# Sliding-window attention with adapters on one core: q and k laid out in 16-row runs, and PSUM handed out by the bank

## The chip, the cores and the metric

The kernel runs on one core of one Trainium2 chip. The metric is the device time of one execution in microseconds. Each execution has a state: "slow" when it lies over 1.5% above the fastest of the same kernel. The engines are called PE (matmuls; PEld is its weight load), ACT, DVE, POOL and SP, as the profile calls them. PE's results land in PSUM; the operands kT and qT of its matmuls lie in SBUF. "Granted clock" is the share of PE's full clock that the profile shows as granted.

## The reference, cut to what matters

```python
# q, k, v: (8 batches, 8 heads, 576 rows, 64)
scores = (q @ k.T) / 8                       # only |row - column| <= 32 survives the mask
attn   = softmax(where(mask, scores, -1e9))
x      = (attn @ v)                          # -> (8*576, 512), heads side by side
# then, per row of x: gate to the best 2 of 8 adapters of rank 16,
out    = x + sum over the 2 of  w * (x @ A[e]) @ B[e]
```

## The kernel before: the parts that matter here

The kernel keeps q and k transposed (64 head columns on partitions, two heads stacked on 128). It loads rows with a DMA that casts to f16, transposes on PE into PSUM, and copies PSUM to SBUF, q on DVE and k on ACT. Rows are loaded in runs of 18 (`NJ`), so a transpose of column block `j` gives every 18th row. The copies put the rows in order. For the score matmul, even and odd keys are kept apart (`v`), and the two stacked heads are interleaved key by key (`t`), with zeros in the other head's places.

```python
NJ, JC = 18, 6
S_t = [psum.tile([128, 2, 512], F32) for i in range(3)]   # 3 buffers of two banks
M_t = [psum.tile([128, 512], F32) for i in range(2)]      # 2 buffers of one bank: all transposes
qT = [const.tile([128, 64 + 4 * S], F16) for i in range(2)]
kT = [const.tile([128, 2, 2 * S, 2], F16) for i in range(2)]     # (v, key pair, t)

def f_q(b, c):      # PSUM -> SBUF on DVE, a third of a batch
    tp  = m16(...)[:, 0:128 * JC].rearrange("p (j r) -> p r j", j=JC)
    dst = qT[b % NQT][:, 32:32 + 4 * S].rearrange("p (r j) -> p r j", j=NJ)
    nc.vector.tensor_copy(out=dst[:, :, JC * c:JC * c + JC], in_=tp)

def f_k(b, c, t, eng):   # PSUM -> SBUF on ACT: 256 groups of 3 elements
    p0  = 64 * t
    tp  = m16(...)[p0:p0 + 64, 0:128 * JC].rearrange("p (h v r) -> p v r h", h=3, v=2)
    dst = kT[b % NKT][p0:p0 + 64, :, :, t].rearrange("p v (r h) -> p v r h", h=9)
    dst = dst[:, :, :, 3 * c:3 * c + 3]
    nc.scalar.copy(out=dst, in_=tp)
...
# A list scheduler in Python fixes the order of all instructions beforehand.
# Each task has an engine, an assumed duration (us), a due time and PSUM buffers:
T["ek", b, c, t] = plan.add("ACT", 0.85, f_k(b, c, t, "ACT"), base + 1 + 0.1 * c, ...)
```

After the scores, ACT takes the exp (`PT`), PE multiplies by v, DVE normalises, and the adapter part follows (transposes of x, gate, two matmuls, copy out).

The softmax here doesn't subtract the row's maximum and nothing guards it: scores larger than these inputs give would overflow.

## Time and profile before

| | before |
|---|---|
| time | 274.05 us (2 runs, 273.84 to 274.26) |
| PE / ACT / DVE busy | 63% / 55% / 42% of 272.8 us |
| kT copies on ACT | 48, 87.7 us in all |
| mean granted PE clock | 0.83 |

The first part of the page gives busy times, and the second one the busy tenths in 40 slices. From the page of the kernel before:

```profile
PE 170.6 (63%) x2312; PEld 120.9 (44%) x2312; DVE 115.2 (42%) x324; ACT 150.8 (55%) x125; POOL 64.4 (24%) x112
...
PE   0203196399529947399539947499439943798642
...
ACT  0007955972497419942696319943696349732413
...
PEclk9999999569956986569956986569959987599987
```

PE and ACT take turns: in seven of the ten slices where ACT shows 9, PE shows 2 to 4 and its clock 5 to 7. Next, groups of instructions (line, engine, operation, output<-input, shapes, count | busy us, mean ns of one | idle time before and what ended it), also from the page before:

```profile
L292 ACT COPY kT<-M 64x768 f16<-64x768 f16 x48 | 87.7, 1826 | 16.0 <-PE M L272 15.3
L322 ACT ACTIVATE PT<-S 128x1024 f16<-128x1024 f32 x36 | 36.8, 1023 | 46.7 <-PE S L312 42.5
...
L281 DVE COPY qT<-M 128x768 f16<-128x768 f16 x24 | 22.4, 951 | 0.1
...
L457 ACT COPY zT<-M 128x640 f16<-128x640 f16 x8 | 5.8, 724 | 22.8 <-PE M L450 22.8
```

A contiguous ACT copy of 640 elements (zT) takes 0.72 us, but the kT copy of 768 takes 1.83 us. The view of waits (who waited for whom: us in total, times, longest) says what PE stood still for:

```profile
PE M L272 <- DVE qT L281: 19.7, 10, 13.0
PE M L379 <- ACT kT L292: 17.0, 4, 5.0
...
PE M L272 <- ACT kT L292: 10.8, 5, 3.1
...
PE S L312 <- ACT kT L292: 8.2, 5, 6.1
```

### The profile page before, as it was taken

The page shows a single profiled execution, that of the slowest core. Times are in us where ns is not written, and L with a number is a line of the kernel's source. Part 1 is how long each engine was busy: PE and PEld are TensorE (multiplying, and loading weights), DVE is VectorE, ACT ScalarE, POOL GpSimd, SP SyncE. Part 2 cuts the span into 40 slices and gives each one's busy share as a digit, 9 for nine tenths or more (in the row PEclk, how much of TensorE's full clock was granted, in tenths as well). Part 3 has the DMA queues.
Part 4 walks back from the last instruction along what each step waited for, and adds up shares of the span by engine and source line. Part 5 has one row for each costly group of instructions (what it writes and reads, how often), then busy time and mean ns, then how long its engine had stood idle before and what let it go on. Part 6 is the DMA issues. An engine that isn't in the chain of part 4 may idle for free. (4 is left out here: it accounts for less than half of the span.)

```text
span 272.8 us, 5487 instructions
## 1 busy us (share of the span) xinstructions
PE 170.6 (63%) x2312; PEld 120.9 (44%) x2312; DVE 115.2 (42%) x324; ACT 150.8 (55%) x125; POOL 64.4 (24%) x112
## 2 busy tenths in 40 slices
PE   0203196399529947399539947499439943798642
PEld 0103074268414833288415833278316721487410
DVE  4883017018811680119801680128803750167430
ACT  0007955972497419942696319943696349732413
POOL 3898643009230041015410031015300000000000
PEclk9999999569956986569956986569959987599987
DMA  6839999009998182908695092909405004000135
GB/s 106 111 34 169 83 140 139 0 2 110 167 118 208 55 106 66 201 20 82 95 130 173 4 118 79 194 2 88 44 2 173 2 2 170 3 4 2 45 129 173
DMA packets 33960, 24.22 MB, mean 89 GB/s; under 512 B 25104, under 2 KB 25232, under 8 KB 33936
## 3 DMA queue, kind: packets, MB, share of 16 engines
q0 software_dynamic: 28688, 14.43, 49.8%
q1 hardware_dynamic: 5248, 9.44, 10.1%
q8 instruction: 18, 0.29, 0.5%
q14 instruction: 6, 0.05, 0.1%
HBM read 28.85 MB, written 9.44 MB: 140 GB/s over the span
## 5 line engine op out<-in xcount | busy, mean ns | idle before, releaser
L292 ACT COPY kT<-M 64x768 f16<-64x768 f16 x48 | 87.7, 1826 | 16.0 <-PE M L272 15.3
L212 POOL DMA_DIRECT2D vbd<-in_v_dram x64 | 38.8, 626 | 101.5 <-PE S L348 94.5
L322 ACT ACTIVATE PT<-S 128x1024 f16<-128x1024 f32 x36 | 36.8, 1023 | 46.7 <-PE S L312 42.5
L272 PE MATMUL M<-ident,r 128*64 128x128 f16 x576 | 28.3, 238 | 37.5 <-DVE qT L281 19.7
L388 DVE COPY xT<-M 128x512 f16<-128x512 f16 x40 | 16.0, 417 | 82.1 <-PE M L379 82.1
L348 PE MATMUL S<-vbd,PT 128*64 128x260 f16 x576 | 44.0, 281 | 0.2
L272 PEld LDWEIGHTS <-r 128*64 128x64 f16 x576 | 23.6, 120 | 43.6 <-issue 35.8
L312 PE MATMUL S<-qT,kT 128*64 128x128 f16 x576 | 35.5, 255 | 8.2 <-ACT kT L292 8.2
L312 PEld LDWEIGHTS <-kT 128*64 128x64 f16 x576 | 30.8, 134 | 21.0 <-ACT kT L292 11.0
L302 PE MATMUL S<-mask,perm 128*64 128x512 f16 x144 | 36.2, 489 | 0.0
L348 PEld LDWEIGHTS <-PT 128*64 128x64 f16 x576 | 33.7, 110 | 3.6 <-ACT PT L322 0.4
L367 DVE TENSOR_TENSOR xs<-S,rc 128x512 f16<-128x512 f32 (+1 forms) x48 | 28.9, 602 | 1.7
L379 PE MATMUL M<-ident,xs 128*128 128x128 f16 x160 | 16.0, 237 | 19.5 <-ACT kT L292 17.0
L364 DVE TENSOR_REDUCE rc<-S 128x8 f32<-128x16 f32 (+1 forms) x48 | 7.9, 166 | 47.0 <-PE S L348 40.0
L468 PE MATMUL S<-B_sb,zT 128*128 128x512 f16 x40 | 23.0, 575 | 6.4 <-ACT zT L457 6.4
L481 ACT COPY obt<-S 128x1024 f32<-128x1024 f32 (+1 forms) x24 | 19.7, 875 | 6.0 <-PE S L470 5.5
L470 PE MATMUL S<-xs,ident 128*128 128x512 f16 x40 | 22.9, 572 | 0.0
L281 DVE COPY qT<-M 128x768 f16<-128x768 f16 x24 | 22.4, 951 | 0.1
L379 PEld LDWEIGHTS <-xs 128*128 128x128 f16 x160 | 10.7, 104 | 23.4 <-issue 21.1
L450 PE MATMUL M<-ident,zs 128*128 128x128 f16 x40 | 4.8, 272 | 24.6 <-DVE qT L281 9.9
L457 ACT COPY zT<-M 128x640 f16<-128x640 f16 x8 | 5.8, 724 | 22.8 <-PE M L450 22.8
L450 PEld LDWEIGHTS <-zs 128*128 128x128 f16 x40 | 3.6, 117 | 25.4 <-issue 16.8
(42 smaller groups left out, 119.4 us busy)
## 6 DMA issues: line engine op xcount, KB each, us to landing
out_dram<-obt SPq DMA_DIRECT2D x24, 256.0 KB, 2.8
r<-in_q_dram POOLq DMA_DIRECT2D x8, 576.0 KB, 6.4
r<-in_k_dram POOLq DMA_DIRECT2D x8, 576.0 KB, 8.6
vbd<-in_v_dram POOLq DMA_DIRECT2D x64, 72.0 KB, 4.1
out_dram<-obt SPq DMA_DIRECT2D x16, 192.0 KB, 2.7
WA_sb<-in_moe_A_dram POOLq DMA_DIRECT2D x4, 32.0 KB, 7.5
B_sb<-in_moe_B_dram POOLq DMA_DIRECT2D x1, 128.0 KB, 4.5
WA_sb<-in_moe_w_gate_dram POOLq DMA_DIRECT2D x4, 2.0 KB, 6.8
```

Source lines behind the costliest of these rows:

```text
L212: nc.gpsimd.dma_start(out=d[64 * uu + t:64 * uu + 64:2, :, VC * c + 1:VC * c + 1 + 2 * D], in_=src)
L272: nc.tensor.matmul(out=tp[64 * t:64 * t + 64, 128 * jj:128 * jj + 128], lhsT=src[:, t, D * j:D * j + D], rhs=ident, is_transpose=True, sta ...
L281: nc.vector.tensor_copy(out=dst[:, :, JC * c:JC * c + JC], in_=tp)
L292: nc.scalar.copy(out=dst, in_=tp)
L302: nc.tensor.matmul(out=pt[64 * uu:64 * uu + 64, 4 * g:4 * g + 4], lhsT=perm[:, 64 * uu:64 * uu + 64], rhs=mask, start=True, stop=False)
L312: nc.tensor.matmul(out=pt[64 * uu:64 * uu + 64, e], lhsT=kT[b % NKT][:, jv, 288 * u + 32 * a:288 * u + 32 * a + 32].rearrange("p r t -> p ...
L322: nc.scalar.activation(out=PT[i % NPT].rearrange("p e w -> p (e w)"), in_=S_t[ps["s", i].slot].rearrange("p g w -> p (g w)"), func=AF.Exp, ...
L348: nc.tensor.matmul(out=po[hh:hh + 64, m // 2 - 2 * gp, :, jv:jv + D + 1], lhsT=PT[i % NPT][:, e, 64 * up:64 * up + 64], rhs=vb[:, a].rearr ...
L367: nc.vector.tensor_tensor(out=xs[b % NX][:, 2 * gp:2 * gp + n, 256 * x:256 * x + 256].rearrange("p g (c d) -> p g c d", c=4), in0=po[:, :, ...
L379: nc.tensor.matmul(out=tp[:, 128 * cc:128 * cc + 128], lhsT=xs[b % NX][:, g, 128 * cc:128 * cc + 128], rhs=ident, is_transpose=True, start ...
L468: nc.tensor.matmul(out=pd[:, i], lhsT=st[b, "zT"][:, g], rhs=B_sb, start=True, stop=False)
L470: nc.tensor.matmul(out=pd[:, i].rearrange("p (t x w) -> p t x w", t=2, x=2), lhsT=ident, rhs=xs[b % NX][:, g].rearrange("p (x t w) -> p t ...
```

## The change

The intent is to make the copies out of PSUM plain. Rows are loaded in runs of 16, half a batch at a time. q stays in the order in which the transposes leave it, (row in the run, group of rows), so that its copy is contiguous and the score matmul reads it in small pieces. k is read contiguously from PSUM too, and the copy's write puts it in key order. The two stacked heads are now 32-element blocks, no longer interleaved. PSUM is one pool of eight banks, q, k and their loads have four buffers, and the preparation of a half batch is due 4 us before its scores. PV matmuls alternate the two halves of the array. The out rows are put back in order by the out DMA.

```diff
-    NJ = 18
-    JC = 6
+    NJ = 16
+    NP = S // NJ
...
-    S_t = [psum.tile([128, 2, 512], F32, name=f"S{i}") for i in range(NS)]
-    M_t = [psum.tile([128, 512], F32, name=f"M{i}") for i in range(NM)]
+    P_t = psum.tile([128, 8, 512], F32, name="P")     # handed out one or two banks at a time
...
-    kT = [const.tile([128, 2, 2 * S, 2], F16, ...) for i in range(NKT)]      # 2
+    kT = [const.tile([128, 2 * NB, 2, 64], F16, ...) for i in range(NKT)]    # 4
...
-    def f_q(b, c):
-            tp = m16(...)[:, 0:128 * JC].rearrange("p (j r) -> p r j", j=JC)
-            dst = qT[...][:, 32:32 + 4 * S].rearrange("p (r j) -> p r j", j=NJ)
-            nc.vector.tensor_copy(out=dst[:, :, JC * c:JC * c + JC], in_=tp)
+    def f_q(y):
+            tp = f16(...)[:, :, 0:576].rearrange("p h (j c) -> p h j c", j=8)
+            dst = qT[...][:, :, 2:2 + 2 * NP].rearrange("p (h j) c -> p h j c", h=2)
+            nc.vector.tensor_copy(out=dst, in_=tp)
...
-    def f_k(b, c, t, eng):        # as above
+    def f_k(y, t, eng):
+            p0 = 64 * t
+            tp = f16(("t", y, 1))[p0:p0 + 64, :, 0:576].rearrange(
+                "p v (j b q) -> p v j b q", j=8, b=18)
+            dst = kT[y % NKT][p0:p0 + 64].rearrange(
+                "p b v (t q j) -> p t v j b q", t=2, q=4)[:, t]
+            for jv in range(2):
+                nc.scalar.copy(out=dst[:, jv], in_=tp[:, jv])     # ACT
...
-                        T["ek", b, c, t] = plan.add("ACT", 0.85, ..., base + 1 + 0.1 * c, ...)
+                    T["ek", y, t] = plan.add("ACT", 1.35, ..., base - 4 + 0.1, ...)   # two copies
```

In the new kT copy the innermost step of the walk is `q`. In kT, one step of `q` is 8 elements, or 16 bytes.

## The prediction

> **What bounds the kernel now.** No engine does: the page's busy shares are PE 63%, ACT 55%, DVE 42%. By the timeline each batch (28 us; first exp at 36 us) is two phases that hardly overlap. In one, ACT copies k out of PSUM: six copies of 1.83 us, about 11 us in a row, while PE starves. The wait view shows PE held by those copies (transposes 10.8 and 17.0 us, scores 8.2, zT transposes 9.5) and by the qT copy (19.7). In the other, PE works and ACT has gaps (exp waits 42.5 us for scores). Two causes: (a) the 48 kT copies take 87.7 of ACT's 150.8 us. A contiguous ACT copy of 640 f16 columns (zT) takes 0.72 us, so 768 columns should take about 0.83 us; these read PSUM in steps of 512 bytes. (b) all transposes share two single-bank PSUM buffers, so k, xT and zT transposes queue behind kT and qT copies, and preparation is due with the scores that need it. The granted clock is 0.83 on average, 0.5 to 0.7 in the k phases.
>
> **What the change does.**
> - k: 64 copies of 576 elements that read PSUM contiguously and write SBUF in 16-byte steps. At zT's rate 0.67 us each, 43 us in all: ACT falls to about 107 us (13.4 per batch). If ACT is slow because of the scattered *write*, they stay at 1.2 to 1.45 us, 77 to 93 us in all, and ACT stays near 140 to 155.
> - q: 24 copies of 0.951 us become 16 contiguous f16 copies, which meet the 2x_1P conditions in the Trainium skill, "Advanced Engine Details and Errata", section "2x-1p Requirements". The trace agrees for xT (512 f16 columns from PSUM in 0.417 us), so I estimate 0.75 us: 22.8 to 12 us.
> - PE: transposes become 1024 instructions, not 576 (estimated +5 us); the PV order alternates array halves without repeats (16 matmuls took 1.04 to 1.10 us; estimated -4 us). Even.
> - Any of eight banks serves any use; loads, q and k go by half batch with four buffers, and preparation is due 4 us before its scores. The phases should overlap.
> - Start: k transposes no longer queue behind qT, which waits for DVE's memsets until 20 us. First exp near 22 us, not 36.
>
> **Sum.** PE's work per batch at full clock, from paces in the trace, is about 16.5 us. With fast k copies PE bounds: 17.5 to 19 us per batch, so 22 + 8 x 18.5 + 10, about 180. With slow copies ACT has 18 to 20 us per batch and about 21 elapse: about 200 to 205. I give the fast copy 65%. Nearly all of the gain is on the critical path: the k phase is.
>
> Predicted: **185 us**, 80% range 165 to 214. Faster by over 2%: 0.96; within 2%: 0.02; slower by over 2%: 0.02.
>
> **What would show it.** kT copies near 0.67 us; qT near 0.75; first exp near 22 us; PE waits on kT and qT nearly gone; mean granted clock above 0.9; PE busy above 75% of the span.
>
> **What would make it wrong.** The kT write (each element in a new 16-byte line, the case that "SBUF — State Buffer", section "Specifications", of the Trainium skill calls penalised; nothing in this trace tests it); score matmuls slowed by reading q in runs of 8 bytes; DMA: all loads in 18 us per batch mean about 165 GB/s written, where slices now peak near 208, and 72-row loads may spread over fewer DMA engines; wrong durations in the static order.

## The result, and the profile after

The changed kernel takes **310.68 us** (2 fast runs, 310.05 to 311.31). Ratios in this document are formed from the fast runs of both kernels in the same rounds, so they are not quite the ratio of the quoted medians. Here the ratio is 1.134, with a 95% interval of 1.123 to 1.144. The change makes the kernel 13% slower. The prediction was 185 us, with a range of 165 to 214.

From the page of the kernel after, the same rows:

```profile
PE 182.1 (59%) x2760; PEld 135.9 (44%) x2760; DVE 105.5 (34%) x297; ACT 228.7 (74%) x141; POOL 77.8 (25%) x136
...
PE   1125373765695638835695638747694728548660
...
ACT  0958878969559797799469797899469796963330
...
PEclk9999585758599575969599576955699566958957
```

```profile
L312 ACT COPY kT<-P 64x576 f16<-64x576 f16 x64 | 166.0, 2837 | 1.9 <-PE P L290 1.7
...
L342 ACT ACTIVATE PT<-P 128x1024 f16<-128x1024 f32 x36 | 37.5, 1043 | 43.7 <-PE P L331 28.9
...
L300 DVE COPY qT<-P 128x1152 f16<-128x1152 f16 x16 | 12.1, 757 | 16.8 <-PE P L290 16.8
```

And the waits of PE in the kernel after:

```profile
PE P L331 <- ACT kT L312: 38.4, 12, 6.4
PE P L322 <- ACT kT L312: 35.4, 12, 5.3
```

The kT copies nearly doubled, from 87.7 to 166.0 us, and each one takes 2.84 us for 576 elements that it reads contiguously. All of ACT's growth is theirs (150.8 to 228.7 us). The q copy did what it should (22.4 to 12.1 us). PE now waits for kT before the mask and score matmuls, 73.8 us in all. The timeline of ACT in the kernel after (start, duration, what, times):

```profile
126.28 15.65 ACT L312 COPY kT<-P 64x576 f16<-64x576 f16 x6
141.44 1.33 ACT L342 ACTIVATE PT<-P 128x1024 f16<-128x1024 f32 x1
...
161.81 10.42 ACT L312 COPY kT<-P 64x576 f16<-64x576 f16 x4
```

Four copies in a row take 10.4 us, so they follow each other every 2.6 us on average. The mean record of 2.84 us is longer because the copies go in pairs, and the record of the first of a pair (2.67 us, the next starts after 2.18) overlaps that of the second (3.00 us). While six run in a row, no exp starts for 15 us.

### The profile page after: what moved, and what is told of

It reads as the page before. It is cut to its first block, busy times and chain, and to the rows that moved or that the text cites. A ratio compares the mean times of both kernels' runs of the same rounds, so it can differ in the third digit from the quotient of the medians.

```text
span 308.1 us, 6466 instructions
## 1 busy us (share of the span) xinstructions
PE 182.1 (59%) x2760; PEld 135.9 (44%) x2760; DVE 105.5 (34%) x297; ACT 228.7 (74%) x141; POOL 77.8 (25%) x136
## 5 line engine op out<-in xcount | busy, mean ns | idle before, releaser
L312 ACT COPY kT<-P 64x576 f16<-64x576 f16 x64 | 166.0, 2837 | 1.9 <-PE P L290 1.7
L322 PE MATMUL P<-mask,ident 128*64 128x512 f16 x144 | 43.0, 529 | 48.2 <-ACT kT L312 35.4
L342 ACT ACTIVATE PT<-P 128x1024 f16<-128x1024 f32 x36 | 37.5, 1043 | 43.7 <-PE P L331 28.9
L331 PE MATMUL P<-qT,kT 128*64 128x128 f16 x576 | 46.7, 277 | 38.4 <-ACT kT L312 38.4
L370 PE MATMUL P<-vbd,PT 128*64 128x260 f16 x576 | 51.0, 317 | 17.2 <-ACT PT L342 8.5
L290 PE MATMUL P<-ident,r 72*64 72x72 f16 x1024 | 26.8, 213 | 7.5 <-DMA r<-in_q_dram 6.3
L388 DVE TENSOR_TENSOR xs<-P,rc 128x512 f16<-128x512 f32 (+1 forms) x48 | 28.9, 602 | 1.7
L290 PEld LDWEIGHTS <-r 72*64 72x64 f16 x1024 | 24.5, 125 | 8.9 <-DMA r<-in_q_dram 6.3
L510 ACT COPY obt<-P 128x1024 f32<-128x1024 f32 (+1 forms) x24 | 19.7, 875 | 11.5 <-PE P L499 11.5
L497 PE MATMUL P<-B_sb,zT 128*128 128x512 f16 x40 | 19.7, 492 | 0.8 <-ACT zT L486 0.8
L300 DVE COPY qT<-P 128x1152 f16<-128x1152 f16 x16 | 12.1, 757 | 16.8 <-PE P L290 16.8
```

Of the source, the lines that this page charges most:

```text
L290: nc.tensor.matmul(out=tp[64 * t:64 * t + 64, s // 8, 72 * (s % 8):72 * (s % 8) + 72], lhsT=src[:, t, D * j:D * j + D], rhs=ident[0:72, 0: ...
L312: nc.scalar.copy(out=dst[:, jv], in_=tp[:, jv])
L322: nc.tensor.matmul(out=pt[64 * uu:64 * uu + 64, 4 * g:4 * g + 4], lhsT=ident[:, 64 * uu:64 * uu + 64], rhs=bcast(mask, 1, 2), start=True, ...
L331: nc.tensor.matmul(out=pt[64 * uu:64 * uu + 64, e].rearrange("p (u j q) -> p u j q", u=2, j=NJ), lhsT=kT[y % NKT][:, NB * uu + a, jv], rhs ...
L342: nc.scalar.activation(out=PT[i % NPT].rearrange("p e w -> p (e w)"), in_=f32(("s", i)).rearrange("p g w -> p (g w)"), func=AF.Exp, scale= ...
L370: nc.tensor.matmul(out=po[hh:hh + 64, m // 2 - 2 * gp, :, jv:jv + D + 1], lhsT=PT[i % NPT][:, e, 64 * up:64 * up + 64], rhs=vb[:, a].rearr ...
```

## The experiments

Three theories were open after the result. Theory W: the copy is slow because of its scattered *write*. Theory R: the copy of the kernel before was slow because of its scattered *read* (my reading in the prediction), and something else slows the new one. Theory P: the copies are a symptom, and the new order of work is at fault.

### e1_write_runs: walk the same copy so that it writes runs

```diff
-            tp = ....rearrange("p v (j b q) -> p v j b q", j=8, b=18)
-            dst = ....rearrange("p b v (t q j) -> p t v j b q", t=2, q=4)[:, t]
+            tp = ....rearrange("p v (j b q) -> p v b q j", j=8, b=18)
+            dst = ....rearrange("p b v (t q j) -> p t v b q j", t=2, q=4)[:, t]
```

The same elements go to the same places; only the order of the walk differs. Writes are now runs of 32 elements, and reads step 144 bytes.

> The kernel after with one edit: each kT copy walks (block, q, j) and not (j, block, q), so that it writes runs of 32 neighbouring f16 (64 bytes) and reads PSUM in steps of 144 bytes. Results stay right. Theory W (ACT is slow because each element it writes lands in a new 16-byte line): the copies fall from 2.84 us to about 0.7 us, and the kernel comes to 175 to 195 us. Rival R (ACT is slow at scattered PSUM reads, as I had read the kernel before): these copies now read scattered, so they cost at least 1.4 us each (2.1 ns per element, as before the change), and the kernel stays above 205 us. Rival P (the copies are not the cause, but the new order of work is): the copies may fall, but the time stays above 270 us.

Measured: 196.67 us median of 4 runs, one of them slow; the three fast ones (195.66 to 197.69, mean 196.3) have a ratio to before of 0.714 (interval 0.709 to 0.718). From its page (the profiled run, 200.96 us):

```profile
L312 ACT COPY kT<-P 64x576 f16<-64x576 f16 x64 | 37.3, 632 | 4.4 <-PE P L290 4.2
```

The copy falls from 2.84 to 0.63 us, and the kernel from 13% more time than before to 29% less. W holds: the scattered read costs nothing here, and the scattered write was the whole excess of this copy. R is out for this copy, and P is out as the main cause. The 196.7 us, and the fast runs too, lie just above the range that was expected.

### e2_before_read_runs: the reverse test, in the kernel before

```diff
-                "p (h v r) -> p v r h", h=3, v=2)
-            dst = kT[...][p0:p0 + 64, :, :, t].rearrange("p v (r h) -> p v r h", h=9)
-            dst = dst[:, :, :, 3 * c:3 * c + 3]
+                "p (h v r) -> p v h r", h=3, v=2)
+            dst = kT[...][p0:p0 + 64, :, :, t].rearrange("p v (r h) -> p v h r", h=9)
+            dst = dst[:, :, 3 * c:3 * c + 3, :]
```

> The kernel before with one edit: each kT copy walks (h, row) and not (row, h), so that it reads PSUM contiguously and writes every element 36 bytes past the last one. Results stay right. Theory W: the copies get slower than their 1.83 us, towards 3.6 us (768 elements at the 4.6 ns that the kernel after shows), and the kernel goes to about 320 to 370 us. Rival R: they fall to about 0.83 us and the kernel gets faster, to 220 to 250 us.

Measured: 350.83 us (4 fast runs), ratio to before 1.275 (1.270 to 1.280). From its view of groups:

```profile
L292 ACT COPY kT<-M 64x768 f16<-64x768 f16 x48 | 165.0, 3438 | 16.0 <-PE M L272 15.3
```

Making the read contiguous and the write scattered takes the old copy from 1.83 to 3.44 us. So for the old copy too the write sets the price, and R is out as its main cause. No run gives the old read in steps of 512 bytes a contiguous write, so a small share of it is not excluded; the count of lines further down leaves little room for one.

### e3_contiguous_floor and e4_pattern_sweep: the floor, and the price by step

e3 replaces the copy by one that is contiguous on both sides; e4 uses eight forms in turn. Both put k in the wrong order on purpose. (The comparison with the reference with these small inputs does not see the order of k. That e1 and e8 are right follows from their walks, which pair the same elements as the kernel after.)

```diff
-            dst = ....rearrange("p b v (t q j) -> p t v j b q", t=2, q=4)[:, t]
+            dst = kT[...][p0:p0 + 64].rearrange("p b v c -> p (b v c)")      # e3
+                nc.scalar.copy(out=dst[:, 576 * jv:576 * jv + 576], in_=tp[:, jv])   # e3, tp contiguous
+   # e4, L312 to L324: o elements apart, o = 2, 4, 8, 16, 32
+                nc.scalar.copy(out=flat[:, 0:576].rearrange("p (i o) -> p o i", o=2),
+                               in_=src.rearrange("p (o i) -> p o i", o=2))
+   # e4, L327 and L330: writes contiguous, reads 8 and 144 bytes apart
+   # e4, L333: runs of 4 elements, 64 bytes apart, reads contiguous
```

> The kernel after with kT copies that read and write contiguously (wrong result on purpose: k lands in the wrong order). This is the floor for the copy: 0.67 us each by zT's rate. Both W and R expect about 175 to 190 us in all; rival P (new order of work at fault) expects more than 270 us.

> The kernel after with eight forms of the kT copy, all of 576 f16 elements on 64 partitions, in turn by half batch and parity (wrong result on purpose; the total time means nothing). Reads contiguous and writes in steps of 4, 8, 16, 32 and 64 bytes; then writes contiguous and reads in steps of 8 and 144 bytes; then runs of 4 elements (8 bytes) every 32 bytes on both sides... reads contiguous. Theory W: the write steps rise from near 0.7 us through about 1.5 to 2.8 us at 16 bytes and stay there beyond it; both scattered reads stay at 0.67 us; runs of 4 are cheap (about 1 us). Rival R: all writes 0.67 us, the read steps 1.4 us and more.

Measured: e3 took 197.77 us (one run, above the 175 to 190 expected) with copies of 632 ns, so e1's copy is at the floor. From e3's view of groups:

```profile
L309 ACT COPY kT<-P 64x576 f16<-64x576 f16 x64 | 37.3, 632 | 4.8 <-PE P L290 4.6
```

e4's view of groups, ACT alone:

```profile
L321 ACT COPY kT<-P 64x576 f16<-64x576 f16 x8 | 23.3, 2912 | 0.0
L318 ACT COPY kT<-P 64x576 f16<-64x576 f16 x8 | 21.7, 2714 | 1.5 <-PE P L290 1.5
L324 ACT COPY kT<-P 64x576 f16<-64x576 f16 x8 | 21.3, 2663 | 1.2 <-PE P L290 1.2
...
L315 ACT COPY kT<-P 64x576 f16<-64x576 f16 x8 | 11.5, 1433 | 0.0
L327 ACT COPY kT<-P 64x576 f16<-64x576 f16 x8 | 7.7, 960 | 0.0
L312 ACT COPY kT<-P 64x576 f16<-64x576 f16 x8 | 6.4, 803 | 2.6 <-PE P L290 2.5
...
L333 ACT COPY kT<-P 64x576 f16<-64x576 f16 x8 | 5.1, 634 | 0.0
L330 ACT COPY kT<-P 64x576 f16<-64x576 f16 x8 | 5.1, 632 | 0.0
```

| write (576 f16 elements) | line | mean ns |
|---|---|---|
| step 4 bytes | L312 | 803 |
| step 8 bytes | L315 | 1433 |
| step 16 / 32 / 64 bytes | L318 / L321 / L324 | 2714 / 2912 / 2663 |
| runs of 4, 64 bytes apart | L333 | 634 |
| contiguous, reads 144 bytes apart | L330 | 632 |

The price nearly doubles with each doubling of the step up to 16 bytes and then stays. That is about what counting 16-byte lines gives: 144, 288 and 576 of them (at a step of 4 bytes the copy takes longer than its 144 lines at 4.5 ns, 0.65 us, so the count is not exact there). Forms of one pair share time in the records, as above: L312, L318, L324 and L330 were always first, the others second, so the 2912 ns of L321 against 2714 of L318 is no sign of a price beyond 16 bytes. (The runs of L333 are 64 bytes apart, not 32 as the expectation says.) The read costs nothing at 144 bytes. The 960 ns of L327 are no price of reading in steps of 8 bytes: L324 and L327 together take 3.15 us from start to start, and with 2.6 us for L324 that leaves about 0.56 us, an estimate, for L327.

### e5_k_copies_on_dve: the same copy on another engine

```diff
-                    eng = ("ACT", "ACT")[t]
+                    eng = ("DVE", "DVE")[t]
```

> The kernel after with its kT copies unchanged in form (contiguous reads, writes in steps of 16 bytes) but run by DVE and not ACT. Results stay right. Theory W1 (the cost of a new 16-byte line is ACT's alone; DVE has no such cost): about 0.72 us per copy, DVE busy near 150 us, the kernel at 200 to 225 us. Theory W2 (every engine pays it at the SBUF write): about 2.6 us per copy, DVE busy near 270 us, the kernel at 300 us or more.

Measured: 341.78 us (one run). From its view of groups, and one row of DVE's timeline:

```profile
L314 DVE COPY kT<-P 64x576 f16<-64x576 f16 x64 | 165.4, 2764 | 2.9 <-PE P L290 2.6
```

```profile
20.80 10.31 DVE L314 COPY kT<-P 64x576 f16<-64x576 f16 x4
```

W2 holds; DVE is busy for 267.8 us. DVE pays the same: four copies in a row take 10.3 us, on ACT 10.4. The two engines differ in their pace for cheap writes (e9's runs of 4 take 0.64 us on ACT and 0.50 on DVE), so the price does not follow either engine's own pace, and moving the copy to DVE does not help.

### e6_plan_told_5us: tell the scheduler what the copies take

```diff
-                    T["ek", y, t] = plan.add(eng, (1.35, 1.35)[t], ...)
+                    T["ek", y, t] = plan.add(eng, (5.2, 5.2)[t], ...)
```

> The kernel after with one number changed: the scheduler is told 5.2 us for a pair of kT copies and not 1.35 us, so that the static order is made for what the chip really takes. Results stay right. Theory W (ACT's work itself is the limit): ACT still has 64 x 2.59 = 166 us of copies and about 63 us of other work, so the time stays between 280 and 312 us, slower than before the change. Rival P (the wrong assumed duration spoils the order, and that is the loss): it falls below 274 us.

Measured: 273.61 us (one run, beside 275.67 of before). Neither theory had this: it lies below what W expected, and so near to the edge of what P did (274) that one run cannot tell on which side. From its page:

```profile
PE 171.8 (63%) x2760; PEld 129.5 (48%) x2760; DVE 106.0 (39%) x297; ACT 225.5 (83%) x141; POOL 77.4 (28%) x136
...
ACT  0886395199999999999999999999999999975040
```

The copies are as slow as ever (2853 ns each), but ACT now works with hardly a gap from the ninth slice on (139.3 of the 140 us from 60 to 200), where the kernel after shows mostly 4 to 9. So of the changed kernel's 310.7 us, about 37 us come from an order that was made for copies of 0.68 us each. The rest is ACT's work itself: 225.5 us of it, in 272.

### e7_before_contiguous_k: how much of the gain is the copy's alone

```diff
-            dst = kT[...][p0:p0 + 64, :, :, t].rearrange("p v (r h) -> p v r h", h=9)
+            dst = kT[...][p0:p0 + 64].rearrange("p v r t -> p (v r t)")
+            dst = dst[:, 128 * JC * c:128 * JC * (c + 1)]       # and tp contiguous; wrong order
```

> The kernel before with kT copies that read and write contiguously (wrong result on purpose): 768 elements in about 0.8 us and not 1.83 us. It splits the gain of e1 into the copy and the rest (half-batch loads, eight shared banks, earlier preparation). If the k phase was ACT's 11 us per batch, this takes 6 us off each of eight batches: 215 to 240 us, and the rest of the change is worth the remaining 20 to 45 us down to e1's 196 us. If the copy was the whole story, about 200 us; if the rest of the change was nearly all, above 250 us.

Measured: 231.32 us (one run, beside 275.67 of before). From its view of groups:

```profile
L291 ACT COPY kT<-M 64x768 f16<-64x768 f16 x48 | 38.1, 793 | 16.7 <-PE M L272 15.6
```

In the kernel before, 48 copies became 1.03 us shorter, 49.6 us in all, and the kernel 44.4 us faster. So about nine tenths of what the copies lose there lay on the critical path. The step from 231.3 to e1's 196.7 us, 35 us, is what the rest of the change is worth once the copy is cheap; which part of it gives how much, no run separates.

### e8_early_start: e1 with an earlier start

In e1 the first score waited 11.6 us for the first q copy, which stood behind DVE's clearing of buffers.

```diff
-    for i in range(1, NKT):
-        nc.vector.memset(kT[i]..., 0)
+    nc.vector.memset(kT[1]..., 0)
     for y in (2, 3):
         load(y, 0)
         load(y, 1)
-        zero_v(y)
-        load_v(y)
-        if y == 2:        # loads of the adapter weights
+        if y == 3:        # loads of the adapter weights
...
+        if y in (2, 3):   # clearing as a DVE task after q copy y - 2; v load and k copy wait for it
+            T["zv", y] = plan.add("DVE", 3.6, (lambda y=y: zero_y(y)), y * W / 2 - 6, [T["eq", y - 2]])
...
-    for s in range(4):    # mask, built by POOL, 0.52 us per instruction
+    for s in range(1):
...
+    for s in range(1, 4):
+        nc.scalar.copy(out=mask[32 * s:32 * s + 32], in_=mask[0:32])
```

(The loads of q and k of half batch 1 also go ahead of the first v load.)

> e1 with an earlier start: DVE clears the v and kT buffers of half batches 2 and 3 after the first two q copies and not ahead of them, the mask is built for 32 partitions and copied to the others by ACT, and the q and k loads of half batches 2 and 3 go ahead of the weights. Results stay right. In e1 the first score waited for the first q copy until 20.9 us (11.6 us of waiting) and later 6.0 us for a q load. Expected: first exp at 14 to 17 us and not 22.9, the load wait gone, the kernel at 183 to 190 us against e1's 196 us. If DMA bounds the first half, the gain at the start is lost again and it stays at 193 to 197 us.

Measured: 184.69 us median of 4 runs, one of them slow; the fast ones are 182.35 to 184.96 (mean 183.9), ratio to before 0.667 (0.659 to 0.674). The first exp in its timeline, and its busy times:

```profile
17.19 1.02 ACT L346 ACTIVATE PT<-P 128x1024 f16<-128x1024 f32 x1 [1.48 <-PE P L335]
```

```profile
PE 144.4 (79%) x2760; PEld 111.4 (61%) x2760; DVE 104.5 (57%) x297; ACT 100.6 (55%) x144; POOL 71.2 (39%) x124
```

The expectation held for the time; the first exp came at 17.2 us, just past the late edge of what was expected, and the later wait for a q load shrank from 6.0 to 2.6 us but did not go. Of the 12 us gained on e1, 5.7 came before the first exp. The rest lies between first and last exp (139.6 us, against 147.2 in e3 and 150.5 in e1's slow run); which of the edits gave it, no run separates. This is the fastest version: a third less time than before.

### e9_line_law and e10_half_words: what exactly is charged

Both are e4's kind of probe (wrong order), with four forms each; the first eight half batches run them on ACT and the last eight on DVE.

```diff
+   # e9:  runs of w elements every s elements, starting at element off
+        out=flat[:, off:off+n*s].rearrange("p (i s) -> p i s", s=s)[:, :, 0:w]
+   #      (w, s, off) = (2, 8, 0) L310, (2, 8, 7) L314, (4, 16, 0) L318, (4, 16, 6) L322
+   # e10: (2, 8, 1) L313;  280 float32 singles every 16 bytes L315;
+   #      560 f16 singles every 4 bytes L317;  280 f16 singles every 16 bytes L319
```

> The kernel after with kT copies of 560 f16 elements, reads contiguous (wrong result on purpose; the total time means nothing), by ACT in the first eight half batches and by DVE in the last eight. Four forms of the write, all with gaps: (1) runs of 2 elements that lie inside a 16-byte line, one run per line; (2) runs of 2 that straddle two lines; (3) runs of 4 inside a line, one in two lines; (4) runs of 4 that straddle (2 + 2). Theory L (a copy takes the longer of its own pace, about 0.62 us, and 4.5 ns for each 16-byte line that it enters): from start to start 1.27, 2.5, 0.63 and 1.27 us on ACT, and on DVE the same apart from its own pace of about 0.7 us. Rival B (the cost goes by the number of separate runs, 280, 280, 140, 140): (1) = (2) and (3) = (4). Rival E (by the number of elements that are not neighbours in one go of the walk, so only single elements are slow): all four near 0.65 us.

> Theory L (a fixed price for each 16-byte line) fell in part: runs of 2 aligned elements, one per line, cost nothing extra. The kernel after again (wrong result on purpose, total time means nothing), ACT in the first eight half batches and DVE in the last eight, reads contiguous. Forms of the write: (1) runs of 2 f16 at an odd element, inside one line, one per line, 280 runs; (2) 280 single float32 in steps of 16 bytes; (3) 560 single f16 in steps of 4 bytes, four per line; (4) 280 single f16 in steps of 16 bytes. Theory H (what costs 4.5 ns is a line that is entered for a half-written 4-byte word; whole words are free): from start to start about 1.3, 0.4, 0.65 to 0.8 and 1.27 us. Rival L (any new line costs, unless its elements come as neighbours): (2) as slow as (4), 1.27 us. Rival N (it is lone elements that cost, neighbours are merged wherever they lie in a line): (1) at 0.65 us, and (2) at 1.27 us.

From the timelines of ACT; each row is four copies in a row, so a quarter of the duration is one copy. e9:

```profile
9.30 2.68 ACT L310 COPY kT<-P 64x560 f16<-64x560 f16 x4
26.80 5.68 ACT L314 COPY kT<-P 64x560 f16<-64x560 f16 x4 [1.15 <-PE P L290]
36.97 2.56 ACT L318 COPY kT<-P 64x560 f16<-64x560 f16 x4 [0.38 <-PE P L290]
46.79 2.70 ACT L322 COPY kT<-P 64x560 f16<-64x560 f16 x4
```

e10:

```profile
9.28 5.64 ACT L313 COPY kT<-P 64x560 f16<-64x560 f16 x4
32.34 3.19 ACT L317 COPY kT<-P 64x560 f16<-64x560 f16 x4 [1.38 <-PE P L290]
46.45 5.68 ACT L319 COPY kT<-P 64x280 f16<-64x280 f16 x4
```

The float32 form, which wrote into a scratch tile, from e10's view of groups (its rows of four took 2.71 and 2.75 us):

```profile
L315 ACT CAST scratch<-P 64x280 f32<-64x280 f16 x8 | 5.3, 665 | 0.8 <-PE P L290 0.7
```

In e9 theory L fell in part: 280 aligned pairs, one to a line, cost 0.67 us and not 1.27; the straddling runs of 2 cost 1.42 and not 2.5. (I had also miscounted there: each line gets the end of one run and the start of the next, so they enter about 280 lines, not 560.) The rival by runs fell too, since forms with equal counts of runs differ, 2.68 against 5.68; and so did E, which had all four forms cheap. e10 separates the rest. A pair at an odd element costs 1.41 us, a pair at an even one 0.67, in as many lines; rival N is out. Lone float32, one to a line, cost 0.67 to 0.69 us where as many lone f16, one to a line, cost 1.42; rival L is out. Theory H is right in kind: a line entered for half of a 4-byte word costs about 5.0 ns (1.41 us over 280 lines). Its "whole words are free" was too much: 280 lone float32 took 0.67 to 0.69 us and not the 0.4 us that I expected, so a whole word in a new line costs at most 2.5 ns. On DVE, rows of four took 5.76 us for L330 of e9 (the straddling pairs) and 5.74 us for L327 of e10 (lone f16), as on ACT.

What stays open is why the hardware charges this; no run shows a mechanism.

## Why the prediction was wrong, point by point

The step that failed is the cost of one kT copy. The prediction had 0.67 us in its main branch and 1.2 to 1.45 us in the other; the trace shows 2.84 us in the records and 2.6 from start to start. So the copies took 166 us of ACT, not 43 or 77 to 93, and ACT was busy for 228.7 us, not 107 or 140 to 155. Where the prediction let 18.5 us per batch pass, or 21 with slow copies, 33.4 passed (from first to last exp).

- **"These read PSUM in steps of 512 bytes."** This was my reason why the old kT copy was slow, and it failed. e2 read contiguously and got slower (3.44 us), e1 reads in steps of 144 bytes and is at the floor (0.632 us). The write was the cause in the new kernel and the main one in the old.
- **"If ACT is slow because of the scattered write, they stay at 1.2 to 1.45 us."** I had this branch, at 35%, but its size was wrong by a factor of two, and with it the range. I had divided the old copy's time by its 768 *elements*. The right divisor was in reach: the old copy wrote groups of three elements 4 bytes apart, every 36 bytes, which by my count enter 384 lines of 16 bytes. 1.826 us over 384 lines is 4.76 ns, and the new copy enters 576 lines: an estimate of 2.74 us. The chip recorded 2.84 us, 2.6 from start to start. (e2's copy enters 768 lines: 3.438 us, 4.48 ns each.) The prediction even cited the Trainium skill, "SBUF — State Buffer", section "Specifications", for the 16-byte line, as a risk, and did not do this division; with "nothing in this trace tests it" it overlooked the old copy.
- **"Wrong durations in the static order"** was named as a risk and not sized. e6 puts it at 37 us: with the true durations the same slow copies take 273.6 us in place of 310.7 (27.4 us per batch in place of 33.4).
- **"Nearly all of the gain is on the critical path: the k phase is."** Right in kind, and it cut the other way. e7 shows that about nine tenths of a saving on the copies reaches the time in the kernel before. The changed kernel's copies cost ACT 78 us more than the old ones. e1 takes 128.7 us off them (166.0 to 37.3), and the kernel gets 114 us faster (310.7 to 196.7 us), the spoilt order included.
- **The fast branch, "about 180".** With the copy repaired (e1), 196.7 us. In e1's profile (a slow run, span 199.0 us) the first exp starts at 22.9 and the last at 173.35 us: 35 steps of 36 tiles, 4.5 tiles to a batch, so 19.3 us per batch against my 18.5. In e3, whose copies are as short and whose time (197.77 us) is close to e1's fast runs, it is 18.9. In both, 25.7 us follow the start of the last exp, where the sum left about 14 (one tile of 4.1 and the 10). The end was the term that was mis-sized most; the kernel before already had 23.1 us there.
- **q.** 0.75 us expected, 0.757 measured, 12.1 us in all. This trace agrees with the Trainium skill, "Advanced Engine Details and Errata", section "2x-1p Requirements": 1152 contiguous f16 take less time than 768 scattered ones did (0.951 us). (Whether the copy ran in the faster mode of that section, the trace does not say.)
- **PE.** The 1024 transposes cost no more than the 576: 32 of them take 0.68 to 0.71 us in the timeline after where the granted clock is high, 12 of the old ones took 0.53. The new PV order gained nothing: 16 matmuls took 1.11 us before and after. Even, as the sum had it, but by luck: both estimates (+5 and -4 us) were wrong.
- **Start.** First exp near 22 us expected, 22.9 measured, although the rest failed.
- **Signs.** Clock above 0.9 and PE above 75% were signs of the fast branch. The kernel after shows 0.76 and 59%; e1's fast runs show 0.93 to 0.94 and e8's 0.96 to 0.97, with PE at 79%. How much of the changed kernel's time is the lower clock's own doing, no run separates.
- **The other two risks.** The score matmuls are not slower for reading q in pieces of 8 bytes: eight take 0.40 us in the timeline after and took 0.42 before. The DMA risk is open. A half-batch load of q lands 6.9 us after its issue (median), and the whole-batch load of before, twice as large, took 6.4. PE waits for q loads for only 6.3 us in the kernel after, before its first transposes, but for 13.0 us in e1.

## What to carry to other kernels

When a copy scatters 2-byte elements, let its walk make runs on the write side and put the scatter on the PSUM read; here that one reordering was worth 114 us of 311. Cost such a copy by the 16-byte lines that it enters and not by its elements: in these runs about 4.5 to 5 ns for each line that is entered for half a 4-byte word, on ACT and on DVE alike. And where a scheduler fixes the order beforehand, feed it measured durations: a wrong one cost 37 us beyond the slow instruction itself.

## What the Trainium skill lacked or had wrong

- "SBUF — State Buffer", section "Specifications", says of the 16-byte cachelines that one needs "≥2 hits per line for full bandwidth". For writes by ACT of single f16 elements two hits per line were far from it: 1433 ns against 632 ns for 576 elements. Four hits gave 803 ns in e4 and, for 560 elements, 0.80 us from start to start in e10; nearly full pace came only with whole words (e9).
- The same page, and "Advanced Engine Details and Errata", section "SBUF Cachelines", speak of a penalty without a size. "Vector Engine (DVE) Microarchitecture Reference", section "Measured stream behaviour on trn2", has sizes, but for 4-byte elements on DVE alone. The runs show one for half words: 4.5 ns per line (576 lines, 2.6 us) to 5.0 ns (280 lines, 1.41 us); where whole words are written, at most 2.5 ns (280 lines, 0.69 us).
- That the price depends on whole or half 4-byte words, and is the same on ACT and DVE (10.4 and 10.3 us for four copies), stands on none of these pages; "SBUF Cachelines" has only that the stride that is tolerated depends on the data type.
- "Advanced Engine Details and Errata", section "PSUM Cachelines", warns of non-contiguous access for matmuls. For an ACT copy, PSUM reads in steps of 144 bytes cost nothing: 632 ns, as contiguous (e1 and e3).
